# An unused 192-byte tile behind the constants: all tiles on the left side of SBUF move up by 192 bytes

## The chip, the cores and the metric

The kernel runs on one core of one Trainium2 chip. The metric is the device time of one execution in microseconds (us); the figure given for a kernel is the median of its runs. Less is better. TensorE (the matrix engine, PE in the profile) multiplies a *moving* operand that streams through it by a *stationary* operand, the weights, that a separate weight load (PEld) brings in ahead of it. Both come from SBUF, the on-chip memory, which has 128 partitions; a tile has the same byte address in each of its partitions.

## The reference

One token-mixing block over x with 2048 tokens and 640 features, all in float32:

```python
g = sigmoid((x * gate_w).sum(-1, keepdims=True))
q, k, v = x @ wqkv                      # 32 heads of 20
phi = lambda t: where(t > 0, t + 1, exp(t)) + 1e-6
kv, z = einsum("bhsd,bhse->bhde", phi(k), v), phi(k).sum(over tokens)
a = (phi(q) @ kv / (phi(q) . z + 1e-6)) @ wo
b = (sigmoid(x @ w_gate) * (x @ w_up)) @ w_down     # 640 -> 1536 -> 640
return g * a + (1 - g) * b
```

## The kernel before

Every float32 factor is split into a high part (rounded to the format that TensorE takes at full rate, `F32R`) and a low part, the rest. A product is then three matmuls that add up in PSUM. This is the helper behind nearly all rows of the profile:

```python
def mm3(out, l_hi, l_lo, r_hi, r_lo, first, last):            # lines 215 to 219
    nc.tensor.matmul(out, l_hi, r_hi, ...)     # L216
    nc.tensor.matmul(out, l_hi, r_lo, ...)     # L217
    nc.tensor.matmul(out, l_lo, r_hi, ...)     # L218
```

`l` is the stationary operand, 128 by 128; `r` the moving one, mostly 128 by 512. In a row `ch<-xth,ws` the output comes first, then the moving and then the stationary tile. Blocks of 2 by 2 are multiplied by a Strassen-like scheme, so that fewer products and more sums are needed; the sums and splits run on VectorE (DVE, helper at L232) and ScalarE (ACT, L228). A Python class `Order` decides at build time in which order these are written down; it knows no addresses. Nothing is scheduled at run time: each engine works through its own list and waits on semaphores.

The stages in order of time are these. (1) From the start to about 143 us the projection of the keys and the Gram matrix of keys and tokens, with matmuls 320 or 322 wide. (2) To about 190 us a mixture with the small per-head matrices (L1251 and others). From there on nearly all matmuls are 512 wide. (3) To about 475 us the first half of the tokens through the feed-forward part: `Block` steps s1 to s7 (up and gate weights `wg`, `wu`, `ws` against the forms of x, `xah`, `xbh`, `xrh`, `xth` and their low parts), and between them ten groups of `down_unit` (hidden values `hf` against the down weights `wd`), and one larger group at the end. (4) To about 658 us the second half of the tokens likewise, with `down_pair` in place of `down_unit` (hidden `hf` against `wf`), cut into smaller pieces that lie between the steps of the blocks. (5) `last_down` (`hf` against `wg`), to 673 us. (6) The attention output: `a_unit` and `ABlock` multiply the scaled queries `pq` and their forms `pt` by the folded matrix M, whose ten tiles (`MHL`) lie partly in a `ws` tile and partly in a `wf` tile (`load_m`).

What matters here is where tiles lie. Pools are stacks: most grow from the left end of SBUF, those opened with `side="right"` from the right end. In the built program the left stack begins with the constants of the pool `common` (the last is `fac`, at byte 10016 of each partition, 8192 bytes long). The next left tile, `gt`, is at 18208. On the left lie among others `xst`, `b12h` and `b12l` of the first half, the first-stage tiles `xn`, `pk`, `kr`, and later `tb`, `wd`, `wf` and most buffers of `hf`. On the right lie the forms of x, `wg`, `wu`, `ws`, `pq`, `pt`, `wst`, the `c` tiles and one buffer of `hf` (at 106464).

Of the operands of 512-wide matmuls, every left one begins 32 bytes past a multiple of 256 (for example 18208 = 71 x 256 + 32, or `wf` at 55072, `hf` at 38688), and every right one 224 bytes past (for example `ws` at 118752, `wg` at 153568). Cuts of these tiles are multiples of 512 bytes, and so leave this as it is. Modulo 512 the numbers are 288 on the left and 480 on the right.

Of the kernel before, what the change touches and what calls it, by code (L numbers as in the profile page):

```python
# [7 lines left out]
F32 = mybir.dt.float32  # L8
# [6 lines left out]
P = 128  # L15
# [178 lines left out]
def gated_mix_kernel(ctx: ExitStack, tc: tile.TileContext, xt, xn, wk, wv, wo, wst_q, wst_f, out_t):  # L194
# [3 lines left out]
    common = ctx.enter_context(tc.tile_pool(name="common", bufs=1))  # L198
# [74 lines left out]
    fac_dram = dram.tile([P, NG, P], F32, name="fac_dram")  # L273
    m_dram = dram.tile([D, D], F32, name="m_dram")
    bdn = HPG * DH

    kp_cm = tc.tile_pool(name="kp", bufs=1)
    kp = kp_cm.__enter__()
# [1995 lines left out]
```

## Time and profile before

| | |
|---|---|
| median of 3 runs | 746.13 us (745.93 to 746.78) |
| the profiled execution's own time | 745.01 us |
| its span, first to last instruction | 743.3 us |
| granted TensorE clock | 1.000 |
| PE busy | 738.5 us, 3626 matmuls |
| DVE, ACT busy | 550.8 us, 330.5 us |

Three things help to read the rows. Matmuls overlap, and their ends are modelled: a row of a 512-wide matmul says 0.39 us, while the next one starts about 0.23 us later. The pace is therefore read from start to start. In a table by stage (`A:B` in us from the span's start, then its length, then each engine's busy time and in brackets the number of instructions), an instruction that was already under way at the stage's start is counted too. Instructions of equal line and tiles that follow each other are merged in a list by time, with their number behind the x.

### The profile page before, as it was taken

The page shows a single profiled execution, that of the slowest core. Times are in us where ns is not written, and L with a number is a line of the kernel's source. Part 1 is how long each engine was busy: PE and PEld are TensorE (multiplying, and loading weights), DVE is VectorE, ACT ScalarE, POOL GpSimd, SP SyncE. Part 2 cuts the span into 40 slices and gives each one's busy share as a digit, 9 for nine tenths or more (in the row PEclk, how much of TensorE's full clock was granted, in tenths as well). Part 3 has the DMA queues.
Part 4 walks back from the last instruction along what each step waited for, and adds up shares of the span by engine and source line. Part 5 has one row for each costly group of instructions (what it writes and reads, how often), then busy time and mean ns, then how long its engine had stood idle before and what let it go on. Part 6 is the DMA issues. An engine that isn't in the chain of part 4 may idle for free.

```text
span 743.3 us, 10191 instructions
## 1 busy us (share of the span) xinstructions
PE 738.5 (99%) x3626; PEld 632.4 (85%) x3626; DVE 550.8 (74%) x968; ACT 330.5 (44%) x622; POOL 107.7 (14%) x174
## 2 busy tenths in 40 slices
PE   9999999999999999999999999999999999999998
PEld 8999999988888888888888888888888888888886
DVE  5888776978577777877877864556777777779976
ACT  5674638248655634333444364344233222223541
POOL 0312112013123311212210211000000031000000
PEclk9999999999999999999999999999999999999999
DMA  8564637789888776667966768977768676559312
GB/s 270 132 176 122 188 68 213 191 270 350 302 313 309 297 261 238 227 239 252 357 261 219 271 196 314 356 220 248 257 254 310 260 218 251 202 213 327 115 65 99
DMA packets 69993, 175.23 MB, mean 236 GB/s; under 512 B 11194, under 2 KB 30410, under 8 KB 66358
## 3 DMA queue, kind: packets, MB, share of 16 engines
q1 hardware_dynamic: 52646, 109.46, 44.4%
q0 software_dynamic: 17152, 64.96, 24.6%
q8 instruction: 28, 0.46, 0.2%
q14 instruction: 23, 0.19, 0.1%
q10 hardware_dynamic: 144, 0.16, 0.1%
HBM read 105.65 MB, written 63.91 MB: 228 GB/s over the span
## 4 chain that ended last, share of the span: by engine, by line
PE 96%; DVE 1%; ACT 1%; DMA 1%; issue 0%; SPq 0%; DVEq 0%
PE ch L216 10%; PE ch L217 10%; PE ch L218 10%; PE dd L218 8%; PE dd L216 8%; PE dd L217 8%; PE cc L216 7%; PE cc L218 7%; PE cc L217 7%; PE rot L216 7%; PE rot L218 6%; PE rot L217 6%; DMA xst<-xt 1%; DVE xst L232 0%; PE rot L304 0%; ACT xth L228 0%
## 5 line engine op out<-in xcount | busy, mean ns | idle before, releaser
L228 ACT ACTIVATE c<-ch 128x512 f32<-128x512 f32 x87 | 52.0, 597 | 168.4 <-PE ch L218 166.5
L232 DVE TENSOR_TENSOR hf<-c,hf 128x512 fp32r<-128x512 f32 x63 | 43.3, 689 | 38.8 <-ACT hf L228 38.7
L232 DVE TENSOR_TENSOR tb<-dd,tb 128x512 f32<-128x512 f32 x73 | 49.8, 688 | 18.0 <-PE dd L218 17.7
L232 DVE TENSOR_TENSOR c<-cc,c 128x512 f32<-128x512 f32 x54 | 37.3, 690 | 32.6 <-ACT c L228 22.5
L228 ACT ACTIVATE c<-c 128x512 f32<-128x512 f32 x57 | 35.9, 629 | 49.4 <-DVE c L232 49.1
L228 ACT ACTIVATE hf<-c 128x512 fp32r<-128x512 f32 x63 | 39.2, 624 | 17.2 <-DVE c L232 16.9
L232 DVE TENSOR_TENSOR tb<-rot,tb 128x512 f32<-128x512 f32 (+1 forms) x61 | 40.9, 679 | 5.8 <-PE rot L218 5.8
L216 PE MATMUL ch<-xth,ws 128*128 128x512 f32 x108 | 42.2, 391 | 0.0
L217 PE MATMUL ch<-xtl,ws 128*128 128x512 f32 x108 | 42.1, 390 | 0.0
L218 PE MATMUL ch<-xth,ws 128*128 128x512 f32 x108 | 42.1, 390 | 0.0
L216 PE MATMUL dd<-xrh,wg 128*128 128x512 f32 x93 | 36.4, 392 | 0.0
L218 PE MATMUL dd<-xrh,wg 128*128 128x512 f32 x93 | 36.3, 390 | 0.0
L217 PE MATMUL dd<-xrl,wg 128*128 128x512 f32 x93 | 36.3, 390 | 0.0
L217 PE MATMUL rot<-pkl,xnh 128*128 128x320 f32 x102 | 31.6, 310 | 0.0
L218 PE MATMUL cc<-xbh,ws 128*128 128x512 f32 x81 | 31.6, 390 | 0.0
L216 PE MATMUL cc<-xbh,ws 128*128 128x512 f32 x81 | 31.6, 390 | 0.0
L217 PE MATMUL cc<-xbl,ws 128*128 128x512 f32 x81 | 31.6, 390 | 0.0
L216 PE MATMUL rot<-pkh,xnh 128*128 128x320 f32 x102 | 31.5, 309 | 0.0
L218 PE MATMUL rot<-pkh,xnl 128*128 128x320 f32 x102 | 31.5, 309 | 0.0
L232 DVE TENSOR_TENSOR c<-c,c 128x512 f32<-128x512 f32 x44 | 30.2, 686 | 1.3 <-ACT c L228 1.0
L228 ACT ACTIVATE ws<-wsum 128x512 fp32r<-128x512 f32 (+1 forms) x24 | 16.2, 680 | 26.9 <-DVE wsum L232 26.9
L216 PEld LDWEIGHTS ch<-xth,ws 128*128 128x128 f32 x108 | 20.3, 188 | 4.5 <-issue 0.3
(563 smaller groups left out, 2271.8 us busy)
## 6 DMA issues: line engine op xcount, KB each, us to landing
wf<-ws POOLq DMA_DIRECT2D x12, 1152.0 KB, 7.0
ws<-wf SPq DMA_DIRECT2D x12, 1152.0 KB, 8.1
wst<-wst_f SPq DMA_DIRECT2D x12, 640.0 KB, 6.4
wf<-wg POOLq DMA_DIRECT2D x12, 640.0 KB, 5.9
wd<-wd POOLq DMA_DIRECT2D x12, 640.0 KB, 6.8
wg<-wf SPq DMA_DIRECT2D x12, 640.0 KB, 6.3
xst<-xt SPq DMA_DIRECT2D x10, 640.0 KB, 7.7
wf<-wd SPq DMA_DIRECT2D x10, 640.0 KB, 5.7
```

The source lines that it names most:

```text
L216: nc.tensor.matmul(out, l_hi, r_hi, start=first, stop=False, skip_group_check=True)
L217: nc.tensor.matmul(out, l_hi, r_lo, start=False, stop=False, skip_group_check=True)
L218: nc.tensor.matmul(out, l_lo, r_hi, start=False, stop=last, skip_group_check=True)
L228: nc.scalar.activation(out, src, fn, **kw)
L232: nc.vector.tensor_tensor(out, a, b, op=op)
```

## The change

It allocates one more tile in the pool of constants and never uses it: 48 float32 in each of the 128 partitions, 192 bytes.

```diff
@@ -273,6 +273,9 @@
     fac_dram = dram.tile([P, NG, P], F32, name="fac_dram")
     m_dram = dram.tile([D, D], F32, name="m_dram")
     bdn = HPG * DH
+
+
+    common.tile([P, 48], F32, name="space")
 
     kp_cm = tc.tile_pool(name="kp", bufs=1)
     kp = kp_cm.__enter__()
```

No instruction reads or writes it. The two built programs have the same 6547 instructions in the same order on each engine, with the same waits and semaphores. Of their 692 SBUF tiles, 335 lie 192 bytes higher: all on the left behind the constants. `gt` moves from 18208 to 18400, `hf` from 38688 to 38880, `wf` from 55072 to 55264. The constants and everything on the right stay. After it, the left operands of 512-wide matmuls begin 224 bytes past a multiple of 256 (18400 = 71 x 256 + 224) and 480 past a multiple of 512, as the right ones did already. In the first stage, where tiles are 2576 bytes long and so begin at many different remainders, left tiles keep their distances to each other, and change it to the right ones.

## The prediction, as it was put on record

> **What bounds the kernel now.** I read the page first (engines and chain), then who waits for whom on TensorE, then the table by stage, and last single stretches of TensorE in order of time.
>
> ```profile
> span 743.3 us, 10191 instructions
> ...
> PE 738.5 (99%) x3626; PEld 632.4 (85%) x3626; DVE 550.8 (74%) x968; ACT 330.5 (44%) x622; POOL 107.7 (14%) x174
> ...
> PE 96%; DVE 1%; ACT 1%; DMA 1%; issue 0%; SPq 0%; DVEq 0%
> ```
> ```profile
> PE rot L304 <- DVE warm L301: 1.3, 1, 1.3
> ```
>
> TensorE is busy for 99% of the span, 96% of the chain that ended last is its own, and the only wait that it is charged with is one of 1.3 us before its first instruction. So the kernel's time is the number of matmuls times the pace at which they start. The change has the same matmuls; only the pace can move. So I looked for stretches in which the pace differs although the shape (128 by 512) is the same and the granted clock is 1.00.
>
> First the reference pace, from ten microseconds in which both operands are on the right side (x forms against `wu`, `ws`, `wg`):
>
> ```profile
> 195.00:205.00 10.00, 10.00 (x46) 1.00 0.86 302
> ```
>
> A row lasts 0.39 us, so about 0.39/0.2267 = 1.7 of the counted matmuls had begun before the window; 46 - 1.7 = 44.3 in 10.00 us is 0.226 us each. I carry 226.7 ns, which the next list confirms over a longer count. It shows a group in which both operands are on the left (`hf`, `wd`), between blocks with both on the right:
>
> ```profile
> 221.61 0.39 PE L216 MATMUL dd<-hf,wd 128*128 128x512 f32 x1
> 221.83 0.39 PE L217 MATMUL dd<-hf,wd 128*128 128x512 f32 x1
> 222.06 0.40 PE L218 MATMUL dd<-hf,wd 128*128 128x512 f32 x1
> 222.30 0.40 PE L216 MATMUL dd<-hf,wd 128*128 128x512 f32 x1
> 222.53 0.39 PE L217 MATMUL dd<-hf,wd 128*128 128x512 f32 x1
> ...
> 224.37 0.39 PE L216 MATMUL dd<-hf,wd 128*128 128x512 f32 x1
> ...
> 228.45 0.39 PE L216 MATMUL ch<-xah,wg 128*128 128x512 f32 x1
> ...
> 229.14 0.39 PE L216 MATMUL ch<-xah,wg 128*128 128x512 f32 x1
> ```
>
> From 221.61 to 224.37 lie 12 matmuls, 230.0 ns each; from 224.37 to 228.45 lie 18, 226.7 ns each. So left against left runs at the same pace as right against right, but only after some ten matmuls of settling, which cost 12 x 3.3 = 0.04 us. The return to the right side costs another 0.01 us (3 matmuls in 0.69 us). No wait stands in these rows; the disturbance comes with the change of side.
>
> Then a stretch with one operand on each side, moving `pq` on the right and stationary `wf` on the left:
>
> ```profile
> 687.85 0.40 PE L218 MATMUL rot<-pq,wf 128*128 128x512 f32 x1
> 688.09 0.39 PE L216 MATMUL rot<-pq,wf 128*128 128x512 f32 x1
> 688.32 0.40 PE L217 MATMUL rot<-pq,wf 128*128 128x512 f32 x1
> ...
> 690.18 0.39 PE L216 MATMUL dd<-pq,ws 128*128 128x512 f32 x1
> ```
>
> Ten matmuls in 2.33 us: 233 ns each, and it never settles. The groups by tile say the same of all such rows (shortest, median and longest duration in ns): mixed sides above, one side below.
>
> ```profile
> L217 PE MATMUL dd<-pq,wf x15: 393/398/399, 677.9 to 717.6; 128*128 128x512 f32 x15
> ```
> ```profile
> L216 PE MATMUL cc<-xbh,ws x81: 388/390/392, 185.8 to 658.3; 128*128 128x512 f32 x81
> ```
>
> The opposite mixture, moving `hf` on the left and stationary `wg` on the right, is the stage of the last down products:
>
> ```profile
> 659.01 0.40 PE L216 MATMUL dd<-hf,wg 128*128 128x512 f32 x1
> ...
> 672.76 0.40 PE L216 MATMUL rot<-pq,ws 128*128 128x512 f32 x1
> ```
>
> Ten output units of six matmuls make 60 in 13.75 us: 229.2 ns each.
>
> The addresses in the built program give these classes a common reading. Left operands begin 32 bytes past a multiple of 256, right ones 224 past. Equal remainders run at 226.7 ns, unequal ones at 229 or 233, and a step from one remainder to the other is followed by a few slow matmuls. The change gives both sides the remainder 224, at which right against right already shows 226.7.
>
> **The change, part by part.** The new tile itself has no instruction, no transfer and no wait: 0, and nothing has to hide it. No step is moved past a queue. What is left is the new pairing, stage by stage, each with the excess over 226.7 ns:
>
> ```profile
> 475.00:658.00 183.00, 183.00 (x803) 150.47 (x802) 132.37 (x209) 57.38 (x100) 14.60 (x26) 1.00 0.70 242
> ...
> 672.77:720.00 47.23, 47.23 (x205) 38.28 (x204) 42.27 (x69) 19.79 (x36) 0.00 (x0) 1.00 0.46 162
> 720.00:735.90 15.90, 15.90 (x71) 12.95 (x70) 14.06 (x27) 5.86 (x12) 0.00 (x0) 1.00 0.22 86
> ```
>
> - 200 to 475 us: ten groups of `down_unit` and the larger last one, each with a change of side in and one out, as in the list above: 11 x (0.04 + 0.01) = 0.55 us.
> - 475 to 658 us, where the down products are cut small and one `hf` buffer is on the right: 803 - 1.7 = 801.3 matmuls would take 181.6 us at 226.7 ns; the stage lasts 183.0: 1.4 us.
> - 659 to 673 us: 60 x (229.2 - 226.7) = 0.15 us.
> - 673 to 720 us, five matmuls on one side and ten on mixed sides in turn: 205 - 1.7 = 203.3 would take 46.1 us; it lasts 47.2: 1.1 us.
> - 720 to 736 us: 71 - 1.7 = 69.3 would take 15.7; it lasts 15.9: 0.2 us.
> - 150 to 190 us, four short groups with `b12h` on the left against `wg`, which by the mixed pace cost about 6 x 5 ns each: 0.1 us. The first stage has some 48 products of a left with a right tile at other remainders: at 6.7 ns each at most 0.3 us, of either sign. I take 0.
>
> Together 3.5 us. By the rows, nothing late takes the place of what goes. TensorE has no charged wait after 1.3 us; VectorE is the next busiest, with 42.27 of 47.23 us (89%) in the stage that gains most, and would have 42.27 of 46.1 (92%), still not full. If single waits came up all the same, each could only give back what its own group had gained, 0.05 us, and not the sum.
>
> [...]
>
> **The rivals.**
>
> *Only steady mixtures gain.* The settling may belong to the change of stage (other PSUM tiles, other lists) and not of side. Then 673 to 736 us (1.1 + 0.2), 0.15 from 659 us and the right `hf` buffer against `wf` remain (by the program's order 33 matmuls at 6.3 ns, 0.2 us): 1.7 us, 744.4 us. Against it: inside the blocks, tiles and PSUM tags change every few matmuls, and the window from 195 to 205 us shows no excess.
>
> *The pace has another cause*, such as the neighbours' accesses in these stages, and the pairing is a coincidence: 746.1 us. For it speaks that sides and stages go together almost everywhere. Against it: left against left settles at 226.7 within the same group.
>
> *Slower: transfers of left tiles lengthen.* The remainder 32 becomes 224 for them, and the right side already has 224. Loads and stores of 640 KB in rows of 2560 bytes, right and left:
>
> ```profile
> wf<-wg POOLq DMA_DIRECT2D x12, 640.0 KB, 5.9
> wd<-wd POOLq DMA_DIRECT2D x12, 640.0 KB, 6.8
> wg<-wf SPq DMA_DIRECT2D x12, 640.0 KB, 6.3
> wf<-wd SPq DMA_DIRECT2D x10, 640.0 KB, 5.7
> ```
>
> A load to the right takes 6.3 us, one to the left 5.7: 10% less. Stores go the other way (5.9 from the right, 6.8 from the left), so the sign is open. If every left transfer took 10% more, it would decide where TensorE is waiting for one, or where the engines are full:
>
> ```profile
> 3.67 0.42 ACT L228 ACTIVATE xah<-xst 128x256 fp32r<-128x256 f32 x1 [1.14 <-DMA xst<-xt]
> ```
> ```profile
> 659.03:672.77 13.74, 13.74 (x62) 11.27 (x61) 9.29 (x16) 6.59 (x12) 0.00 (x0) 1.00 0.99 376
> ```
>
> The first load ends at 3.67 us: at most 0.3 us later. At a DMA share of 0.99 a tenth more is 1.4 us, once the loads for the next stage land behind their first use. With no gain from the pairing, 746.1 + 1.7 = 747.8 us. With the gain it would be 744.3.
>
> [...]
>
> **How the numbers follow.** The sum is made against the profiled execution: 745.01 us, of which 743.3 are the span and 1.7 lie around it. It would take 741.5. The median of the runs shown is 1.1 us above that execution, and I carry the difference: 746.13 - 3.5 = 742.6 us. I give the pairing 0.71, only steady mixtures 0.10, another cause 0.12, longer transfers 0.07. The range reaches from the full sum with 0.3 us from the first stage and half a microsecond of scatter (the three runs span 0.85 us), 741.8, to the second case with as much scatter above it, 744.9; outside lie 0.19 of the two last cases. About 0.2% (1.5 us) is what a measurement of this kernel can tell from no change, so faster means under 744.6: 0.71 and 0.09 of the second case, 0.80. Slower (over 747.6) is the last case, 0.07. The rest is 0.13.
>
> **What would show it.** In the profile after, 475 to 658 us would be about 1.4 us shorter for the same matmuls; the ten `pq,wf` matmuls would take 2.27 us instead of 2.33, and their median duration would fall from 398 to about 390 ns; the first twelve matmuls of a `hf,wd` group would take 2.72 us instead of 2.76. If these stay and the time falls, the theory is wrong. If they come and the time doesn't fall, a wait on VectorE or a transfer has taken their place, and would be charged to TensorE. A mixed pace that is only less slow would mean that more than the remainder of 256 counts.

## The result, and the profile after

| | before | after |
|---|---|---|
| median | 746.13 us (745.14 to 746.78, 5 runs) | 742.56 us (742.10 to 744.16, 5 runs) |
| profiled execution | 745.01 us, span 743.3 | 743.42 us, span 741.7 |

The ratio is 0.9958 (95% interval 0.9943 to 0.9972): the kernel became faster by 3.6 us, or 0.4%. The forecast was 742.6.

First the page of the changed kernel, its span and its engines:

```profile
span 741.7 us, 10191 instructions
...
PE 735.2 (99%) x3626; PEld 631.6 (85%) x3626; DVE 550.2 (74%) x968; ACT 330.3 (45%) x622; POOL 107.1 (14%) x174
```

Count and share are the same, and TensorE still bounds the kernel; it needs 3.3 us less for the same 3626 matmuls. The ten matmuls with moving `pq` (right) and stationary `wf` (left), from the list by time (start, duration):

```profile
687.31 0.39 PE L218 MATMUL rot<-pq,wf 128*128 128x512 f32 x1
687.54 0.39 PE L216 MATMUL rot<-pq,wf 128*128 128x512 f32 x1
...
689.58 0.39 PE L216 MATMUL dd<-pq,ws 128*128 128x512 f32 x1
```

They take 2.27 us, 227 ns each, instead of 2.33. The groups by tile (shortest, median, longest duration in ns) say so of the whole stage, and of the opposite mixture:

```profile
L217 PE MATMUL dd<-pq,wf x15: 389/389/389, 677.6 to 716.3; 128*128 128x512 f32 x15
...
L216 PE MATMUL dd<-hf,wg x10: 389/389/389, 659.0 to 670.5; 128*128 128x512 f32 x10
```

Where 393/398/399 stood, there is now one duration. The start of a `hf,wd` group after a block, which was the settling:

```profile
223.55 0.39 PE L216 MATMUL dd<-hf,wd 128*128 128x512 f32 x1
223.77 0.39 PE L217 MATMUL dd<-hf,wd 128*128 128x512 f32 x1
...
226.27 0.39 PE L216 MATMUL dd<-hf,wd 128*128 128x512 f32 x1
```

Twelve matmuls take 2.72 us instead of 2.76, 226.7 ns each from the first on. The table by stage (length, then busy us and in brackets the count of PE, PEld, DVE, ACT, POOL; granted clock, DMA share, GB/s):

```profile
475.00:658.00 183.00, 183.00 (x809) 151.54 (x808) 133.44 (x211) 57.38 (x100) 14.59 (x26) 1.00 0.71 245
...
672.77:720.00 47.23, 47.23 (x210) 39.08 (x210) 43.26 (x71) 21.14 (x37) 0.00 (x0) 1.00 0.47 167
```

In the same 183.00 us lie 809 matmuls instead of 803, and (809 - 1.7) x 0.22667 = 183.0: no excess is left. In the same 47.23 us lie 210 instead of 205, and (210 - 1.7) x 0.22667 = 47.2. VectorE is at 43.26 of 47.23, the 92% that the forecast gave it, and takes nothing back.

The profiled execution of after shows only 1.6 us less span than that of before, not 3.6. One group of each end of the 512-wide part, of before and then of after (the times behind the durations are the starts of the first and last of the group), shows where the rest is:

```profile
L216 PE MATMUL dd<-hf,wd x60: 389/390/398, 221.6 to 416.0; 128*128 128x512 f32 x60
...
L218 PE MATMUL rot<-hf,wf x42: 279/394/399, 492.2 to 739.5; 128*128 128x512 f32 x40, 128*128 128x256 f32 x2
```
```profile
L216 PE MATMUL dd<-hf,wd x60: 389/389/389, 223.5 to 417.3; 128*128 128x512 f32 x60
...
L218 PE MATMUL rot<-hf,wf x42: 279/389/389, 493.5 to 737.9; 128*128 128x512 f32 x40, 128*128 128x256 f32 x2
```

From the first to the last, 517.9 us became 514.4: 3.5 us less. But this execution reached the first of them 1.9 us later. Its waits on TensorE (total us, times, longest), and those behind the first instruction of another execution of the same program, run `e7_again` below:

```profile
PE rot L307 <- DVE warm L304: 1.3, 1, 1.3
PE rot L216 <- DVE gt L232: 1.0, 1, 1.0
PE cc L216 <- ACT ms L228: 0.4, 1, 0.4
PE cc L216 <- ACT b12h L228: 0.3, 1, 0.3
```
```profile
PE cc L216 <- ACT ms L228: 1.2, 1, 1.2
PE ch L216 <- DVE k1h L594: 0.3, 1, 0.3
```

The first pays 1.7 us after its start, 1.0 of it on `gt` near 62 us; the second doesn't wait there at all, but 1.2 us on `ms` near 171 us. These waits of the first 200 us change from one execution to the next, and the same program has medians of 742.56 and 742.28 us.

### The profile page after: what moved, and what is told of

Its sections match the earlier page's. It is cut to its first block, busy times and chain, and to the rows that moved or that the text cites. A ratio compares the mean times of both kernels' runs of the same rounds, so it can differ in the third digit from the quotient of the medians.

```text
span 741.7 us, 10191 instructions
## 1 busy us (share of the span) xinstructions
PE 735.2 (99%) x3626; PEld 631.6 (85%) x3626; DVE 550.2 (74%) x968; ACT 330.3 (45%) x622; POOL 107.1 (14%) x174
## 4 chain that ended last, share of the span: by engine, by line
PE 91%; DMA 3%; DVE 2%; ACT 2%; issue 0%; SPq 0%; DVEq 0%
PE ch L216 10%; PE ch L217 9%; PE ch L218 9%; PE dd L217 8%; PE dd L216 8%; PE dd L218 8%; PE cc L216 7%; PE cc L218 7%; PE cc L217 7%; PE rot L216 6%; PE rot L217 6%; PE rot L218 6%; DMA xst<-xt 3%; DVE xst L232 1%; ACT xth L228 0%
## 5 line engine op out<-in xcount | busy, mean ns | idle before, releaser
L232 DVE TENSOR_TENSOR c<-ch,c 128x512 f32<-128x512 f32 x24 | 16.5, 687 | 9.9 <-PE ch L218 9.9
```

Of the source, the lines that this page charges most:

```text
L232: nc.vector.tensor_tensor(out, a, b, op=op)
```

## The experiments

All edits are made in the kernel before, behind the line `bdn = HPG * DH`. The excess given with each run of the whole kernel is worked out from its trace: of all 2535 matmuls 512 wide, the time from start to start beyond 226.667 ns, added up (gaps over 250 ns, taken for waits, left out). It was 3.91 us before and 0.35 after.

**The other side moved instead.**

```diff
+    gap_r = ctx.enter_context(tc.tile_pool(name="gap_r", bufs=1, side="right"))
+    gap_r.tile([P, 48], F32, name="space_r")
```

> The kernel before with 192 unused bytes at the right end of SBUF instead of the left: every right tile moves down by 192 bytes to 32 past a multiple of 256, where the left ones already are; nothing on the left moves. Pairing theory (equal remainders of the two operands give 226.7 ns per matmul): the same gain as the change, 742 to 743 us, and the pq,wf matmuls at a median row of 389 to 390 ns. Rival, the place of the left tiles as such (remainder 224 is good, 32 is bad): no gain, 746 us or, with both sides now at 32, more. Rival, coincidence: 746 us.

Measured: 743.05 us (742.07 to 744.08), ratio to before 0.9958 (0.9947 to 0.9970), a hair above the 742 to 743 us that were expected. Here all right tiles lie 192 bytes lower and the left ones stay, so that both sides have the remainder 32. Groups by tile:

```profile
L217 PE MATMUL dd<-pq,wf x15: 389/389/389, 676.6 to 715.3; 128*128 128x512 f32 x15
...
L216 PE MATMUL dd<-hf,wg x10: 389/389/389, 658.0 to 669.6; 128*128 128x512 f32 x10
```

The excess is 0.33 us. The gain doesn't come with a place on the left or with the remainder 224, but with equal remainders.

**Both sides moved.**

```diff
+    common.tile([P, 48], F32, name="space")
+    gap_r = ctx.enter_context(tc.tile_pool(name="gap_r", bufs=1, side="right"))
+    gap_r.tile([P, 48], F32, name="space_r")
```

> Both shifts at once: left tiles at 224 past a multiple of 256, right ones at 32, the two remainders exchanged. Pairing theory: unequal again, so the gain goes, 745.5 to 746.5 us; the two mixed paces are exchanged, about 229 ns for pq on wf and about 233 ns for hf on wg. Rival, the place of the left tiles as such: they lie as in the changed kernel, 742 to 743 us. Rival, longer transfers from remainder 224: no statement on the pace.

Measured: 745.47 us (744.81 to 746.61), ratio 0.9989 (0.9981 to 0.9998). The left now has 224 and the right 32. Groups by tile:

```profile
L216 PE MATMUL dd<-pq,wf x15: 394/394/394, 678.8 to 718.0; 128*128 128x512 f32 x15
L217 PE MATMUL dd<-pq,wf x15: 388/388/388, 679.0 to 718.2; 128*128 128x512 f32 x15
...
L217 PE MATMUL dd<-hf,wg x10: 394/394/394, 660.2 to 672.1; 128*128 128x512 f32 x10
```

Each edit alone brings 3 us or more, both together bring 0.7. From start to start all `pq,wf` run at 229.5 ns (before 233.2) and `hf,wg` at 233.1 (before 229.3): the two mixtures have exchanged their paces, with tiles, partners and neighbours as they were. By stage, the excess falls from 1.14 to 0.52 us between 673 and 720 us, where `pq,wf` is, and rises from 0.15 to 0.39 between 659 and 673, where `hf,wg` is. What counts is therefore the difference with its sign, moving minus stationary modulo 256: 192 gives 233, 64 gives 229.

**The left moved to a distance of 128.**

```diff
+    common.tile([P, 16], F32, name="space")
```

> The unused tile with 64 bytes instead of 192: left tiles at 96 past a multiple of 256, right ones at 224, 128 apart. Pairing theory with a period of 256 bytes or more: still unequal, 745 to 747 us. Pairing theory with a period of 128 or 64 bytes and 32-byte steps within it: 128 apart counts as equal, 742 to 743 us. Coincidence: 746 us.

Measured: 745.36 us (744.75 to 748.23), ratio 0.9990 (0.9982 to 0.9998).

```profile
L217 PE MATMUL dd<-pq,wf x15: 392/392/395, 679.1 to 718.8; 128*128 128x512 f32 x15
...
L216 PE MATMUL dd<-hf,wg x10: 392/398/398, 660.0 to 671.9; 128*128 128x512 f32 x10
```

Both mixtures run at 233 (233.7 and 233.1 ns). Half the period is no remedy for a mixture; what little was gained (excess 3.10) lies in the stages with many changes of side, 0.64 to 0.27 us from 200 to 475 us and 1.27 to 0.77 to 658 us, since settling is shorter at a step of 128 (one slow interval against ten at a step of 64, last experiment).

**A tile of the same kind that keeps the remainder.**

```diff
+    common.tile([P, 64], F32, name="space")
```

> The unused tile with 256 bytes: all left tiles move as with the change, even further, but their remainder of 256 stays 32. Pairing theory: the time of the kernel before, 745.5 to 746.7 us, with the mixed paces of before (pq on wf about 233 ns, hf on wg about 229 ns). Rival, any move of the left side helps or costs something (overlaps with the right side, other waits): a time that differs from before.

Measured: 746.28 us (745.36 to 747.16), ratio 1.0000 (0.9991 to 1.0008).

```profile
L217 PE MATMUL dd<-pq,wf x15: 393/398/398, 678.7 to 718.4; 128*128 128x512 f32 x15
...
L217 PE MATMUL dd<-hf,wg x10: 388/388/397, 660.1 to 671.8; 128*128 128x512 f32 x10
```

Moving the left by 256 bytes changes nothing (excess 3.89; 233.2 and 229.4 ns). That a tile is added, and that everything behind it moves, is no cause.

**Equal modulo 256, unequal modulo 512.**

```diff
+    common.tile([P, 112], F32, name="space")
```

> The unused tile with 448 bytes, 192 + 256: remainders of both sides are equal modulo 256 (224), but differ modulo 512 (left 224, right 480). Pairing theory with a period of 256 bytes: the gain of the change, 742 to 743 us, pq on wf at 226.7 ns. With a period of 512 or more: no gain, about 746 us.

Measured: 742.15 us (741.35 to 742.49), ratio 0.9942 (0.9930 to 0.9954).

```profile
L217 PE MATMUL dd<-pq,wf x15: 389/389/389, 676.3 to 715.1; 128*128 128x512 f32 x15
```

Excess 0.33 us: 256 is the period; 512 isn't needed.

**The changed kernel once more**, beside the two last ones.

```diff
+    common.tile([P, 48], F32, name="space")
```

> The changed kernel once more, unaltered, for a second profile of it. In the first one TensorE waited 1.0 us for gt near 62 us and reached the 512-wide stages 2 us later than in the profile of before. If that is scatter between executions, this profile is without the wait, and its span is 1 to 2 us shorter; if the shift causes it (left tiles are loaded later, or new pairs of remainders in the first stage), the wait is there again.

Measured: 742.28 us (741.83 to 742.94), ratio 0.9946 (0.9935 to 0.9958). It can't be told from 742.15. The wait on `gt` is gone, as scatter would have it, but the span is only 0.5 us shorter (741.7 to 741.2) and not the 1 to 2 us expected, because this execution waits 1.2 us on `ms` in its place.

**The pace by itself.** A program of its own, which leaves out the whole computation: only 512-wide matmuls in `F32R`, 30 for each pair of remainders, while no other engine works.

```python
for m, w in combos():            # all 8 x 8 remainders in steps of 32, then finer ones
    for i in range(30):
        nc.tensor.matmul(ps[...], wt[:, at remainder w + 512 * (i % 8)],
                                  mv[:, at remainder m + 2048 * (i % 3)], ...)
```

> The pace by itself: another program, which leaves out the whole computation and runs only matmuls, 30 in a row (128 by 512, the same F32R format) for each of 64 pairs of remainders of the moving and the stationary operand (0, 32 .. 224 past a multiple of 256), and then some finer and coarser offsets. No other engine works meanwhile. Pairing theory: 226.7 ns where the remainders are equal, about 233 ns where moving minus stationary is 192, about 229 ns where it is 64, and the pace depends on the difference alone. Rival, place as such: the pace depends on one of the two remainders, not on the difference. Rival, accesses of the other engines: 226.7 ns everywhere. Unknown to all: whether some difference is faster than equal.

One profiled execution. Windows from the start of one group to the start of the next, for moving and stationary at (64, 64), (0, 224), (0, 192) and (0, 64); the counts include matmuls already under way:

```profile
146.36:153.17 6.81, 6.81 (x32) 1.00 0.00 0
69.78:76.78 7.00, 7.00 (x31) 1.00 0.00 0
62.90:69.78 6.88, 6.88 (x31) 1.00 0.01 2
34.91:41.91 7.00, 7.00 (x31) 1.00 0.01 2
```

30 matmuls each: 227.0, 233.3, 229.3 and 233.3 ns, the few of settling among them. Worked out from the starts of the 13th to the 30th of each group, in ns:

```
moving minus stationary, modulo 256   settled pace
0 (all 8 pairs)                       226.6 to 226.7
32                                    233.3 to 233.4
64                                    228.7 to 228.9
96, 160, 192, 224                     233.1 to 234.1
128                                   232.2 to 233.6
moving further by 256, 512 or 1024, or stationary by 256:  226.6
stationary further by 4, 8, 16 bytes: 232.1, 230.6, 233.4
moving further by 4, 8, 16 bytes:     238.4, 233.3, 231.5
```

With VectorE and ScalarE silent and a DMA share of 0.01 at most, the classes of the kernel stand there again: 0 at 226.7, 64 (`hf,wg` before) at 229, 192 (`pq,wf` before) at 233.5. The pace goes by the difference: each class holds eight pairs, one for each remainder of the moving operand. Nothing that was tried was faster than equal remainders, so no better padding was found.

**Settling, alternation, width and type.** A second program of this kind; it too leaves the computation out.

> The pace by itself again, in a program that leaves out the whole computation, 30 matmuls for each case. (1) Equal pairs whose common remainder changes from case to case (0, 192, 0, 64, 0, 128, 0, 32): 226.7 ns once settled, and, if the settling belongs to the change of remainder, about ten slower matmuls after each change; without that, the settling in the kernel belongs to the change of stage. (2) Remainders that alternate from matmul to matmul. If the moving stream is disturbed by the weight load that runs beside it, that of the next matmul, then pairs that are equal within each matmul but alternate between matmuls are slow, and pairs that are unequal within a matmul but equal to the next one's weights run at 226.7 ns. If a matmul's own weights count, it is the other way round. (3) 320 wide at differences 0, 64, 128, 192, 32: by the sum of the first stage in the traces (147.3 ns on the mean in all four kernels) the difference should matter little there. (4) bf16 operands at the same differences: unknown.

One profiled execution. Windows from start to start: after a step of the common remainder from 0 to 64, back from 64 to 0, and from 0 to 128; then 30 matmuls 320 wide at the differences 0 and 64.

```profile
42.44:49.28 6.84, 6.84 (x31) 1.00 0.00 0
```
```profile
49.28:56.10 6.82, 6.82 (x31) 1.00 0.00 0
56.10:62.91 6.81, 6.81 (x31) 1.00 0.00 0
```
```profile
118.20:122.59 4.39, 4.39 (x31) 1.00 0.00 0
122.59:126.99 4.40, 4.40 (x33) 1.00 0.01 4
```

At 226.7 ns thirty matmuls take 6.80 us. The steps add 0.04, 0.02 and 0.01 us. The single intervals, in ns, from the starts:

```
step 0 -> 64, this program       229 229 233 236 224 231 236 227 234 230 | 227 226 227
step 192 -> 0, this program      228 229 233 236 224 231 236 228 233 231 | 226 227 227
right -> left, kernel before     228 230 233 236 224 231 236 228 232 231 | 227
step 64 -> 0, this program       229 233 230 | 227 227
step 0 -> 128, this program      231 | 227 226
```

From right to left the common remainder goes from 224 to 32, which modulo 256 is a step of 64 like the first two. The sequence of the kernel returns without its stages, PSUM tags or neighbours: settling belongs to the step of the remainder. And 320 wide, every difference tried (0, 32, 64, 128, 192) runs at 146.5 to 146.7 ns. In bfloat16, 512 wide, the same differences run at 215.8 to 215.9 ns.

In the same program remainders alternated from matmul to matmul. With 0 and 64 on both operands in step the pace is about 232 ns, with 0 and 64 against 64 and 0 it is 233; with 0 and 128, 228 and 230; with 0 and 192, 232 and 233. If only a matmul's own weights counted, the first of each two numbers would be 226.7; if only the weights being loaded for the next one counted, the second would. Neither is. The test is not a clean one, since the remainder takes a step at every matmul, and settling runs through all of it.

## Why the prediction was right, point by point

**TensorE's pace is the time.** Right. The medians fell by 3.57 us and the excess by 3.91 - 0.35 = 3.56 us. That the two agree to 0.01 us, and that the median came out within 0.1 us of the forecast, is luck: the interval of the ratio allows 2.1 to 4.3 us, and the five runs spread from 742.10 to 744.16 us. The excess is the firmer measure. The kernels line up the same way: excess 0.33 to 0.35 in those at 742.2 to 743.1 us, 3.33 and 3.10 at 745.5 and 745.4, 3.89 at 746.3.

**Equal remainders modulo 256 decide.** Shown: two edits on opposite sides make them equal, and each gives the whole gain; done together they don't; 256 bytes do nothing; and the pace program has the classes with no kernel around it. The reading of the trace of before, left against left settling at 226.7 ns inside one group, pointed to it. It could not tell 256 from 512, and the forecast had no need to, since the change makes both sides equal modulo 512 as well; the tile of 448 bytes told them apart.

**The terms of the sum.** The excess over the same matmuls, by the stages of the forecast:

```
stage in us     forecast   before   after   gone
150 to 190       0.1        0.35     0.23    0.12
200 to 475       0.55       0.64     0.07    0.57
475 to 658       1.4        1.27     0.00    1.27
659 to 673       0.15       0.15     0.00    0.15
673 to 720       1.1        1.14     0.00    1.14
720 to 736       0.2        0.31     0.00    0.31
all 512 wide     3.5        3.91     0.35    3.56
```

What stays up to 190 us after the change are slow intervals of 512-wide matmuls with equal remainders, behind gaps and behind the small matrices (from 153.09 us: 235, 233, 236, 224, 231, 236 ns), much like those of settling.

Two terms were off by 0.1 us, in opposite directions, and so cancelled, which is luck too. In 475 to 658 us the forecast took length minus count as excess, and so counted a gap as pace:

```profile
526.36 0.39 PE L218 MATMUL cc<-xbh,ws 128*128 128x512 f32 x1
526.63 0.47 PE L216 MATMUL ch<-xth,ws 128*128 128x512 f32 x1
526.94 0.40 PE L217 MATMUL ch<-xtl,ws 128*128 128x512 f32 x1
```

These start 0.27 and 0.31 us apart with both operands on the right: 0.12 us over the pace. The trace names no wait there. After shows no such gap at this place, but `e1`, with equal remainders too, has one again (0.42 and 0.31 us, from 526.2), so it is not the pairing's. The stage did become 1.4 us shorter (182.95 to 181.56), but not all of that is the gain of equal remainders. In 720 to 736 us it is the edges of the window: 69 matmuls start in it, all 512 wide, and from the first of them to the start behind the last lie 15.95 us, 0.31 us more than 69 x 0.22667. The forecast set 69.3 of them against 15.90 us.

**The first stage was taken as 0.** Right in pace, for a reason that the forecast didn't have. It allowed 0.3 us for some 48 products by the 512-wide price; but 320 wide none of the five differences tried has a price, as the second program shows. The mean of the kernel's own matmuls 320 and 322 wide (waits left out) is 147.39 ns before and 147.32 after. Its scatter is the larger matter: the profiled executions reach one and the same matmul (the first `dd<-xrh,wg` behind 198 us) at 198.5 us before, 200.4 after, 199.2, 199.7, 200.4, 199.4, 199.2 and 200.0 in `e1` to `e7` (without `e4`), where the kernel that adds 256 bytes has 199.4. Whether the moved addresses cost a few tenths of that can't be settled from single executions, nor from the medians with their interval of 2.1 to 4.3 us.

**Only steady mixtures gain** fell: the stretch from 200 to 475 us, which has only settling, gave up its 0.57 us, and the second program repeats the settling. By the addresses in the built program, only 269 of the 2535 matmuls 512 wide were mixed before (181 at the difference 192, 88 at 64), and they held 1.5 of the 3.91 us of excess; 2.4 us lay in matmuls with equal remainders, and 2.1 of these went with the changes of side. In this kernel the changes of side cost more than the mixtures themselves. **The pace has another cause** fell: the classes run with every other engine silent. There a class at 233.5 ns stands beside one at 226.7, with nothing but the two addresses changed. Through what part of the hardware the addresses act, no run shows.

**Transfers of left tiles lengthen** was the rival on the slower side. DMA issues of the changed kernel (KB each, median us to landing), then of the first experiment, in which the right tiles have gone from remainder 224 to 32:

```profile
wf<-wg POOLq DMA_DIRECT2D x12, 640.0 KB, 5.9
wd<-wd POOLq DMA_DIRECT2D x12, 640.0 KB, 6.9
wg<-wf SPq DMA_DIRECT2D x12, 640.0 KB, 5.6
wf<-wd SPq DMA_DIRECT2D x10, 640.0 KB, 5.6
```
```profile
wg<-wf SPq DMA_DIRECT2D x12, 640.0 KB, 6.8
```

With remainder 224 loads to the left take 5.6 us (before 5.7) and stores from it 6.9 (6.8). The load to the right, which stayed where it was, went from 6.3 to 5.6, and with remainder 32 it took 6.8; but in the second profile of the changed kernel, with nothing different, it took 6.9. These rows scatter by more (5.6 to 6.9 us for one and the same program) than any effect of the remainder that they show, and the 10% that the rival asked for is not in them.

**What stays open.** Why the remainder modulo 256 matters, no run shows. The page of after has weight loads busy for 631.6 us and matmuls for 735.2 in a span of 741.7, so the two overlap most of the time; that they disturb each other there unless their addresses keep step is the author's guess. It would fit the difference with its sign and the settling. Whether a matmul's own weights or those of the next one count, the alternating runs didn't settle.

## What to carry to other kernels

Where TensorE is full, read its pace from start to start, and compare stretches of equal shape by where their operands lie: a few per cent that no wait explains can be a matter of addresses (here up to 3%, 233.5 beside 226.7 ns). For 512-wide `F32R` matmuls, give the moving and the stationary tile the same remainder modulo 256 (226.7 ns here, where the other differences in steps of 32 bytes ran at 228.7 to 234.1); where one pool grows from the left end of SBUF and another from the right, one unused tile of less than 256 bytes can do it for all at once (here 192 bytes, 746.13 to 742.56 us), as long as the cuts of the tiles are multiples of 256 bytes. A single profiled execution can hide such a gain behind scatter elsewhere (here 1.6 us of span for 3.6 us of median): compare the same instructions, from the first to the last that the change touches.

## What the runs showed of the hardware that was not expected

- The price has no order: of the differences in steps of 32 bytes, 64 costs 2 ns (228.7 to 228.9 beside 226.7), all others 6 to 7, and half the period (128, at 232.2 to 233.6) is as bad as the rest.
- Four bytes are enough: the moving operand 4 bytes further runs at 238.4 ns, the slowest of all; the stationary one 4 bytes further at 232.1.
- After a step of the common remainder the pace settles in a fixed sequence, ten intervals for a step of 64 (from 0 to 64 as from 192 to 0), three back, one for 128.
- Width and type decide whether it matters at all: 320 wide in `F32R` (146.5 to 146.7 ns) and 512 wide in bfloat16 (215.8 to 215.9 ns) are indifferent to the addresses tried. Even at equal remainders `F32R` takes 226.7 ns, 5% more than bfloat16, so its rate is not quite the highest that TensorE showed.
